# Batch 5's strided output goes through DRAM with an earlier deadline, and the Exp parts beside MM2 groups are spread out again

## The chip, the cores and the metric

The kernel runs on one core of a Trainium2 chip. A core has a matrix engine (TensorE, written PE in the profile, with its weight loads as PEld), a vector engine (DVE), a scalar engine (ACT), a general engine (POOL), and a sync engine (SP) that issues most DMAs here. Each engine runs its own instructions in order; they wait for one another through semaphores. The metric is the device time of one execution in microseconds (us); lower is better. Verdicts come from several runs of both kernels on one chip.

## What is computed

An attention with 8 heads over 8 batches of 576 positions, followed by a two-layer network with a squared ReLU:

```
B, H, S, D = 8, 8, 576, 64          # inputs q, k, v, float32
mask_local   = (rel >= 0) & (rel < 32)                    # heads 0 to 3, rel = i - j
mask_strided = (rel >= 0) & (j % 32 == i % 32)            # heads 4 to 7
attn = softmax(where(mask, q @ k.T / 8, -1e9));  o = attn @ v
x   = o as [B*S = 4608, H*D = 512]
h   = x @ w_in                      # w_in  512 x 2048
out = (max(h, 0) ** 2) @ w_out      # w_out 2048 x 512
```

The kernel leaves out all score blocks that a mask makes empty: a local row sees its own block of 96 and the 32 keys before it; a strided row sees only the 18 keys of its class modulo 32, so 4 classes make a block of 72.

## The kernel before

**Units.** A unit `u` is one batch and one pair of heads; batch b has units 4b to 4b+3. The first two are local, the last two strided. The output of a pair fills one of the four arrays `xt[0..3]` (128 rows of two heads, 4608 columns of positions), which is the transposed x that the network reads. `xt[2]` and `xt[3]` hold the strided pairs; batch b's columns are 576b to 576b+575.

**Steps of a unit.** `step_T` transposes q or k on PE (early batches only; later ones come transposed by DMA). `step_S` makes the scores: four banks of PSUM out of the five of pool `ps_t`, then four Exp parts on ACT (`expo(row, half)`) and two mask multiplications on DVE (`masks(row)`). `step_D` multiplies by v, in two or three parts, and scales by the row sums, giving `x_l` or `x_s` in SBUF, with positions on the partitions. Last, this x must be transposed into `xt`. There are three ways: `step_E` on PE with a copy by DVE or ACT (L449 to L460); for local pairs from batch 2 on a DMA transpose from SBUF (L444); and for strided pairs for which `by_dram` holds, `step_X`: SP writes `x_s` to a DRAM tile `x_d` (L471), and six groups later SP issues a DMA transpose from there to `xt` (L473).

**Groups.** The network is cut into nine chunks of 512 columns, and each chunk into 16 pieces of MM1 (`mm1`: four matmuls, one on each `xt[kk]` in turn, then ReLU on ACT and the square on DVE) and 16 of MM2 (`mm2`: four matmuls; every fourth one ends with a copy of y on ACT and a store on SP). These 288 pieces, of four matmuls each, are the groups; they are listed in a fixed order. Chunks 0, 1 and 2 have their 16 MM1 groups, and chunks 0 and 1 their 16 MM2 groups, in stretches of one kind; from chunk 3 on MM1 of one chunk alternates with MM2 of the chunk before. MM2 of chunks 0 and 1 are groups 16 to 31 and 48 to 63. MM1 of chunk c from 3 on starts at group 80 + 32(c-3); chunk 5 starts at group 144, chunk 6 at 176.

**The plan.** The attention steps are spread over the groups so that batch b's are done by a deadline. Batch b must be there when chunk b starts. The deadline is two groups before that, or 14 groups before for batches from XD on; this is read from the constant `XD` in two places:

```
    def by_dram(u):
        return not is_local(u) and units[u][0] >= XD
...
        g_end, s_end = ready.get(b, starts[b] - (14 if b >= XD else 2)), ends[4 * b + 3]
...
        if b + 2 < B:
            plan(b + 2, g_end + 2, g_prev, g_end)
```

So the deadlines are groups 110, 142, 162 and 194 for batches 4, 5, 6 and 7. The last line hangs the loads of batch b+2 on the same stretch: `loads_qk` at 45% of it (loads of local q and k by SP, casts of strided q and k to DRAM by POOL's DMAs, casts by POOL), `transpose_str` (SP's two DMA transposes of strided q and k, which wait for those casts) at 80% of it or 8 groups after the first, `transpose_local` (two DMA transposes for each local pair) 14 and 18 groups after the first, and `loads_v` two groups after the deadline (four DMAs for local v, two for strided v, and POOL's casts).

**The parts of a score step.** `later(n, ...)` puts work n groups off. Normally the four Exp parts and the masks of a pair are spread over four groups, so that ACT can serve the ReLUs between them. In the kernel before, `free_act` is set in MM2 groups of chunks 0 and 1, where there are no ReLUs; a score step there issues its four Exp parts at once, and its masks one and two groups later.

Of the kernel before, what the change touches and what calls it, by code (L numbers as in the profile page):

```python
# [14 lines left out]
def kernel(  # L15
# [79 lines left out]
    def is_local(u):  # L95
        return units[u][1] < H // 4
# [140 lines left out]
        nc.gpsimd.dma_start(out=w_out_b[:, c, :], in_=w_out_v[:, c, :])  # L237

    clock = [0]
    free_act = [False]  # L240
    pending = []

    def later(n, fn, key=None):
        pending.append((clock[0] + n, key, fn))
# [8 lines left out]
    def tick():  # L253
        clock[0] += 1
        run_due(lambda x: x[0] <= clock[0])
# [36 lines left out]
    def step_S(u):  # L292
        s = st[u]
        qT, kT = s["qT"], s["kT"]
        local = is_local(u)
        w, n = (QL, NL) if local else (SP_, NJ)
        kn = 128 if local else SP_
        hn = n // 2
        e = es[u % 4]
        s["e"] = e  # L300
        banks = [[None, None], [None, None]]
        for half in range(2):
            for row in range(2):
                banks[row][half] = ps_t.tile([128, 512], FP32, name="pt")
            for i in range(hn):
                t = half * hn + i
                klo = w * t
                for row in range(2):
                    rows = slice(64 * row, 64 * row + 64)
                    if not local and units[u][0] >= XB:  # L310
                        c0 = w * (t // 4)
                        lhsT, rhs = (a[rows, t % 4, c0:c0 + w] for a in (kT, qT))
                    else:
                        lhsT, rhs = kT[rows, klo:klo + kn], qT[rows, w * t:w * (t + 1)]
                    nc.tensor.matmul(banks[row][half][0:kn, w * i:w * (i + 1)], lhsT, rhs,  # L315
                                     start=True, stop=True)

        def expo(row, half):
            lo = S * row + S // 2 * half
            nc.scalar.activation(e[0:kn, lo:lo + S // 2], banks[row][half][0:kn, 0:S // 2],  # L320
                                 AF.Exp, scale=scale)

        def masks(row):
            x = e[0:kn, S * row:S * (row + 1)].rearrange("p (t c) -> p t c", c=w)
            m = mask_loc if local else mask_str
            nc.vector.tensor_tensor(x, x, m.to_broadcast([kn, n, w]), op=ALU.mult)  # L326
            if u < 2:
                nc.vector.memset(x[0:32, 0], 0.0)

        s["masks"] = masks  # L330
        if units[u][0] == 0:
            for row, half in ((0, 0), (0, 1), (1, 0), (1, 1)):
                expo(row, half)
            return
        if free_act[0]:
            for row, half in ((0, 0), (0, 1), (1, 0), (1, 1)):
                expo(row, half)
            later(1, lambda: masks(0), u)
            later(2, lambda: masks(1), u)
            return  # L340
        expo(0, 0)
        later(1, lambda: expo(0, 1), u)
        later(2, lambda: (masks(0), expo(1, 0)), u)
        later(3, lambda: expo(1, 1), u)
        later(4, lambda: masks(1), u)
# [114 lines left out]
                                  px.rearrange("c (j p) -> c p j", j=NJ))  # L460
        st.pop(u)

    XD = 6

    def by_dram(u):
        return not is_local(u) and units[u][0] >= XD

# [11 lines left out]
    def mm1(c, ff, kks=range(4), order=range(4), pool=None):  # L479
        if ff == 0 and c not in gs:  # L480
            gs[c] = g_pool.tile([128, 16, 512], BF16, name="g_sb")
        g = gs[c]
        if kks[0] == order[0]:
            phs[ff] = ph_tile() if pool is None else pool.tile([128, 512], FP32, name="py")
        ph = phs[ff]
        for kk in kks:
            nc.tensor.matmul(ph, w_in_b[:, kk, 128 * ff:128 * (ff + 1)],  # L487
                             xt[kk][:, 512 * c:512 * (c + 1)],
                             start=(kk == order[0]), stop=(kk == order[-1]))
        if kks[-1] != order[-1]:  # L490
            return
        r = r_pool.tile([128, 512], BF16, name="r")
        nc.scalar.activation(r, ph, AF.Relu)  # L493
        later(1, lambda: nc.vector.tensor_tensor(g[:, ff, :], r, r, op=ALU.mult))  # L494
# [3 lines left out]
    def mm2(c, i, pool=None):  # L498
        j, part = divmod(i, 4)
        g = gs[c]  # L500
        if part == 0:
            ys[c, j] = ps_y.tile([128, 512], FP32, name="py") if pool is None else ph_tile()
        py = ys[c, j]
        for ff in range(4 * part, 4 * part + 4):
            nc.tensor.matmul(py, g[:, ff, 128 * j:128 * (j + 1)], w_out_b[:, ff, :],  # L505
                             start=(ff == 0), stop=(ff == 15))
        if part == 3:
            y = y_pool.tile([128, 512], FP32, name="y")
            r0 = 512 * c + 128 * j
            if r0 + 128 == T:  # L510
                nc.vector.tensor_copy(y[:, 0:256], py[:, 0:256])
                nc.scalar.copy(y[:, 256:512], py[:, 256:512])
                nc.sync.dma_start(out=out[r0:r0 + 128, 0:256], in_=y[:, 0:256])
                nc.scalar.dma_start(out=out[r0:r0 + 128, 256:512], in_=y[:, 256:512])
                return
            nc.scalar.copy(y, py)  # L516
            nc.sync.dma_start(out=out[r0:r0 + 128, :], in_=y)

    T_ = lambda u, nm: (lambda: step_T(u, nm))
    S_ = lambda u: (lambda: step_S(u))  # L520
    D_ = lambda u, part: (lambda: step_D(u, part))
    E_ = lambda u: (lambda: step_E(u))
# [12 lines left out]
    def first_steps():  # L535
# [14 lines left out]
        for item in (("T", a, "q"), 2, ("T", a, "k"), 2, ("T", b, "q"), ("S", a), 1, ("T", b, "k"), 2, ("S", b),  # L550
                     ("M", a), 1, ("T", c, "q"), ("T", c, "k"), 1, ("N", a), ("S", c), 1, ("M", b), ("N", b), 1,
                     ("T", d, "q"), ("T", d, "k"), 2, ("S", d), 1, ("M", c), ("N", c), ("O", b), 1, ("X", b),
                     ("O", a), 1, ("M", d), ("X", a), ("N", d), ("O", c), ("X", c), ("P", (b, a), (0,)), ("O", d),
                     ("P", (b, a), (1, 2)), ("X", d), ("P", (c,)), ("P", (d,))):
            if isinstance(item, int):
                warm(item)
                continue
            op, u = item[0:2]
            if op == "T":
                step_T(u, item[2])  # L560
            elif op == "S":
                step_S(u)
            elif op == "M":
                masks(u)
            elif op == "N":
                step_N(u)
            elif op == "O":
                outs(u)
            elif op == "X":
                scaled[u]()  # L570
            else:
                part(*item[1:])
# [128 lines left out]
    groups = []  # L701
    starts = {}
    weights = []
    only_mm2 = []

    def add(c, kind, i, pool=None):
        only_mm2.append(kind == 2 and c < 2)
        if kind == 0:
            groups.append(lambda: None)
            weights.append(3)  # L710
        elif kind == 1:
            if i == 0:
                starts[c] = len(groups)
            groups.append(lambda: mm1(c, i))
            weights.append(3 if c < 3 else 5)
        else:
            groups.append(lambda: mm2(c, i, pool))
            weights.append(7 if c < 2 else 5)

    def mm1_alone(c):  # L720
        for i in range(16):
            add(c, 1, i)

    for ff in range(16):
        add(0, 1, ff) if ff >= NP else add(0, 0, ff)
    for part in range(4):
        for j, pool in ((0, ps_h), (1, ps_h), (2, None)):
            add(0, 2, 4 * j + part, pool)
# [35 lines left out]
    for b in range(1, B):  # L764
        g_end, s_end = ready.get(b, starts[b] - (14 if b >= XD else 2)), ends[4 * b + 3]
        if b == 1:
# [6 lines left out]
        done_prev, g_prev = s_end, g_end  # L773
    done = 0
    for n, g in enumerate(groups):
        free_act[0] = only_mm2[n]
        while done < due[n]:
            steps[done]()
            done += 1
        for fn in hooks.get(n, ()):  # L780
            fn()
        g()
        tick()
# [32 lines left out]
```

## Time and profile before

| what | value |
|---|---|
| median of 3 runs | 314.05 us (313.89 to 314.37) |
| the profiled execution, its own time | 314.05 us |
| its span, from first to last instruction | 312.3 us |
| granted TensorE clock, mean | 1.000 |
| matmuls of MM1 (L487) and MM2 (L505) | 576 + 576, 379 ns each as recorded, overlapping |
| Exp parts (L320) | 128, 407 ns each |
| PE transposes of x (L451) | 80 of strided x, 12 of local x |
| copies of strided xt by DVE (L459) | 6, 750 ns each |
| writes of x_d (L471), issue on SP | 4, 309 to 334 ns |
| transposes from x_d (L473), issue on SP | 4, 1175 to 1187 ns |

A recorded matmul of 379 ns overlaps its neighbours: four of them, one group, follow each other in 0.86 us on the chain. The chain of waits is the way to read this kernel: for each stretch it tells what the next instruction waited for. SP's own timeline tells when each DMA was issued; its "us" are the issue alone, not the transfer.

### The profile page before, as it was taken

The page shows a single profiled execution, that of the slowest core. Times are in us where ns is not written, and L with a number is a line of the kernel's source. Part 1 is how long each engine was busy: PE and PEld are TensorE (multiplying, and loading weights), DVE is VectorE, ACT ScalarE, POOL GpSimd, SP SyncE. Part 2 cuts the span into 40 slices and gives each one's busy share as a digit, 9 for nine tenths or more (in the row PEclk, how much of TensorE's full clock was granted, in tenths as well). Part 3 has the DMA queues.
Part 4 walks back from the last instruction along what each step waited for, and adds up shares of the span by engine and source line. Part 5 has one row for each costly group of instructions (what it writes and reads, how often), then busy time and mean ns, then how long its engine had stood idle before and what let it go on. Part 6 is the DMA issues. An engine that isn't in the chain of part 4 may idle for free.

```text
span 312.3 us, 6165 instructions
## 1 busy us (share of the span) xinstructions
PE 299.5 (96%) x2352; PEld 146.8 (47%) x2352; DVE 165.9 (53%) x411; ACT 162.3 (52%) x337; POOL 90.6 (29%) x117
## 2 busy tenths in 40 slices
PE   8889899999999999999999999999999999999994
PEld 3544455545554544444444454444444444444441
DVE  7676656578766866577466657654432222222200
ACT  3966554577555765555555555555444444444311
POOL 8518852727730633291057025000000000000000
PEclk9999999999999999999999999999999999999999
DMA  7999999999999999999899885224132000000111
GB/s 142 157 206 221 206 191 246 190 283 232 182 179 206 199 222 171 185 239 234 165 208 214 168 186 112 73 71 55 52 93 66 34 37 34 34 34 36 67 67 67
DMA packets 92172, 44.99 MB, mean 144 GB/s; under 512 B 76592, under 2 KB 85456, under 8 KB 91952
## 3 DMA queue, kind: packets, MB, share of 16 engines
q1 hardware_dynamic: 77120, 34.09, 51.2%
q0 software_dynamic: 14880, 10.39, 22.7%
q8 instruction: 18, 0.29, 0.4%
q10 hardware_dynamic: 144, 0.13, 0.1%
q14 instruction: 10, 0.08, 0.1%
HBM read 36.70 MB, written 13.57 MB: 161 GB/s over the span
## 4 chain that ended last, share of the span: by engine, by line
PE 76%; DMA 9%; DVE 6%; POOL 5%; issue 1%; ACT 1%; DVEq 0%; POOLq 0%; ACTq 0%
PE ph L487 32%; PE py L505 27%; PE ph L505 9%; DMA w_in_b<-in_moe_w_in_dram 4%; PE pt L419 3%; DMA qT_s<-in_q_dram 3%; PE pt L315 3%; DVE x_s L434 2%; DMA kTl<-k_l 1%; DVE g_sb L494 1%; PE pt L451 1%; POOL vs L227 1%; DVE e L326 1%; DVE kTl L286 1%; ACT r L493 1%
## 5 line engine op out<-in xcount | busy, mean ns | idle before, releaser
L487 PE MATMUL ph<-xt,w_in_b 128*128 128x512 bf16 x572 | 143.7, 379 | 0.3 <-ACT r L493 0.3
L493 ACT ACTIVATE r<-ph 128x512 bf16<-128x512 f32 x143 | 85.3, 597 | 94.6 <-PE ph L487 93.7
L494 DVE TENSOR_TENSOR g_sb<-r 128x512 bf16<-128x512 bf16 x144 | 69.9, 488 | 106.0 <-ACT r L493 105.1
L505 PE MATMUL py<-w_out_b,g_sb 128*128 128x512 bf16 x400 | 102.7, 379 | 0.0
L487 PEld LDWEIGHTS <-w_in_b 128*128 128x128 bf16 x576 | 52.3, 98 | 56.4 <-issue 0.5
L505 PEld LDWEIGHTS <-g_sb 128*128 128x128 bf16 x576 | 52.4, 98 | 55.2
L320 ACT ACTIVATE e<-pt 128x288 bf16<-128x288 f32 (+1 forms) x128 | 46.4, 407 | 14.8 <-PE pt L315 14.7
L505 PE MATMUL ph<-w_out_b,g_sb 128*128 128x512 bf16 x176 | 42.8, 379 | 0.0
L419 PEld LDWEIGHTS <-e 128*128 128x128 bf16 (+1 forms) x392 | 20.8, 97 | 15.9 <-issue 0.6
L192 POOL CAST vl<-vl_st 128x768 bf16<-128x768 f32 x12 | 10.6, 880 | 50.5 <-DMA vl_st<-in_v_dram 42.4
L434 DVE TENSOR_TENSOR x_s<-pt,rinv 72x384 bf16<-72x384 f32 (+1 forms) x42 | 21.4, 509 | 1.4
L326 DVE TENSOR_TENSOR e<-e,mask_str 72x576 bf16<-72x576 bf16 x32 | 17.1, 539 | 6.0 <-ACT e L320 5.9
L123 POOL CAST q_l<-q_st 96x768 bf16<-96x768 f32 x14 | 12.3, 877 | 24.8 <-DMA q_st<-in_q_dram 14.8
L326 DVE TENSOR_TENSOR e<-e,mask_loc 128x576 bf16<-128x576 bf16 x32 | 16.8, 525 | 3.5 <-ACT e L320 3.3
L516 ACT COPY y<-py 128x512 f32<-128x512 f32 x25 | 14.7, 587 | 5.5 <-PE py L505 5.5
L123 POOL CAST k_l<-k_st 96x768 bf16<-96x768 f32 x14 | 13.6, 974 | 11.6 <-DMA k_st<-in_k_dram 9.7
L434 DVE TENSOR_TENSOR x_l<-pt,rinv 96x384 bf16<-96x384 f32 x28 | 15.5, 553 | 1.0
L433 DVE RECIPROCAL rinv<-pt 96x6 f32<-96x6 f32 (+2 forms) x70 | 12.8, 183 | 5.1 <-PE pt L419 4.8
L516 ACT COPY y<-ph 128x512 f32<-128x512 f32 x10 | 5.9, 590 | 17.0 <-PE ph L505 17.0
L208 POOL CAST vs<-v_st 72x1024 bf16<-72x1024 f32 x12 | 14.0, 1197 | 0.4
L419 PE MATMUL pt<-vs,e 72*128 72x65 bf16 x224 | 13.1, 193 | 0.0
L530 PE MATMUL py<-y 128*128 128x512 bf16 x24 | 9.5, 485 | 1.3 <-DVE y L659 1.3
(87 smaller groups left out, 157.7 us busy)
## 6 DMA issues: line engine op xcount, KB each, us to landing
out_dram<-y SPq DMA_DIRECT2D x35, 256.0 KB, 3.4
vl_st<-in_v_dram SPq DMA_DIRECT2D x24, 144.0 KB, 3.9
v_st<-in_v_dram SPq DMA_DIRECT2D x12, 288.0 KB
q_st<-in_q_dram SPq DMA_DIRECT2D x16, 144.0 KB, 4.3
k_st<-in_k_dram SPq DMA_DIRECT2D x16, 144.0 KB, 6.8
w_in_b<-in_moe_w_in_dram POOLq DMA_DIRECT2D x4, 512.0 KB, 12.5
w_out_b<-in_moe_w_out_dram POOLq DMA_DIRECT2D x4, 512.0 KB, 10.8
q_st<-in_q_dram SPq DMA_DIRECT2D x7, 288.0 KB, 8.5
```

Source lines behind the costliest of these rows:

```text
L123: copy(t.rearrange("p j h d -> p h j d"), s[name + "f"].rearrange("p h (j d) -> p h j d", j=6))
L208: (copy or nc.gpsimd.tensor_copy)(t[:, :, 0:D], s["vf"].rearrange("p h (j d) -> p (h j) d", d=D))
L320: nc.scalar.activation(e[0:kn, lo:lo + S // 2], banks[row][half][0:kn, 0:S // 2], AF.Exp, scale=scale)
L326: nc.vector.tensor_tensor(x, x, m.to_broadcast([kn, n, w]), op=ALU.mult)
L419: nc.tensor.matmul(po[:, n - n0, :], e[0:kn, pos(n):pos(n) + 128], rhs[0:kn, src(n), 0:D + 1], start=True, stop=True)
L433: nc.vector.reciprocal(rinv[0:w, 0:m], po[0:w, 0:m, D:D + 1])
L434: nc.vector.tensor_tensor(x, po[0:w, 0:m, 0:D], rinv[0:w, 0:m].to_broadcast([w, m, D]), op=ALU.mult)
L487: nc.tensor.matmul(ph, w_in_b[:, kk, 128 * ff:128 * (ff + 1)], xt[kk][:, 512 * c:512 * (c + 1)], start=(kk == order[0]), stop=(kk == order ...
L493: nc.scalar.activation(r, ph, AF.Relu)
L494: later(1, lambda: nc.vector.tensor_tensor(g[:, ff, :], r, r, op=ALU.mult))
L505: nc.tensor.matmul(py, g[:, ff, 128 * j:128 * (j + 1)], w_out_b[:, ff, :], start=(ff == 0), stop=(ff == 15))
L516: nc.scalar.copy(y, py)
```

## The change

```
@@ the spreading of Exp parts and masks
-    free_act = [False]
...
-        if free_act[0]:
-            for row, half in ((0, 0), (0, 1), (1, 0), (1, 1)):
-                expo(row, half)
-            later(1, lambda: masks(0), u)
-            later(2, lambda: masks(1), u)
-            return
         expo(0, 0)
         later(1, lambda: expo(0, 1), u)
         later(2, lambda: (masks(0), expo(1, 0)), u)
         later(3, lambda: expo(1, 1), u)
         later(4, lambda: masks(1), u)
@@ the way of strided x
-    XD = 6
+    XD = 5
@@ the list of groups, and the loop over them
-    only_mm2 = []
...
-        only_mm2.append(kind == 2 and c < 2)
...
-        free_act[0] = only_mm2[n]
```

The first part is undone everywhere: score steps beside MM2 groups of chunks 0 and 1 (seven of them, of batches 1 and 3) spread their parts like all others. The second part moves units 22 and 23 (batch 5, strided) from `step_E` to `step_X`, and batch 5's deadline from group 142 to 130. With it the steps of batch 5 lie in groups 110 to 130 and those of batch 6 in 130 to 162 (before 110 to 142 and 142 to 162). The loads of batch 7, which hang on batch 5's stretch, move too: `loads_qk` from group 124 to 119, `transpose_str` from 135 to 127, the two `transpose_local` from 138 and 142 to 133 and 137, `loads_v` from 144 to 132. Nothing changes in what is computed. POOL's instructions keep their order.

## The prediction

> **What bounds the kernel now.** I read first the shares and slices of the page:
>
> ```profile
> PE 299.5 (96%) x2352; PEld 146.8 (47%) x2352; DVE 165.9 (53%) x411; ACT 162.3 (52%) x337; POOL 90.6 (29%) x117
> PE   8889899999999999999999999999999999999994
> DMA  7999999999999999999899885224132000000111
> ```
>
> PE has no free slice from 120 us to its end at 308 us, so there a step on PE costs its length and a wait of PE is lost for good. The DMA engines are full until about 170 us. Next the chain of waits, in the stretch where batch 5 ends:
>
> ```profile
> 167.49 0.26 PE pt L451 x8
> 175.63 0.26 PE pt L451 x8
> 177.62 0.18 PE pt L419 x6
> 177.80 0.86 PE ph L487 x4
> 179.71 0.40 PE pt L315 x16
> ```
>
> All pieces are PE's. The two L451 rows are step E of units 22 and 23. Counting four matmuls to a group, the L487 at 177.80 is group 144, the first MM1 of chunk 5, which reads batch 5's xt. Then SP's timeline, since the new DMAs go through SP in order:
>
> ```profile
> 155.97 1.21 SPq L444 DMA_TRANSPOSE xt<-x_l  x1
> 157.28 0.53 SPq L517 DMA_DIRECT2D out_dram<-y  x1
> 157.86 1.40 SPq L107 DMA_DIRECT2D q_st<-in_q_dram  x2
> 163.10 1.38 SPq L107 DMA_DIRECT2D k_st<-in_k_dram  x2
> 164.57 1.26 SPq L444 DMA_TRANSPOSE xt<-x_l  x1
> 165.94 0.54 SPq L517 DMA_DIRECT2D out_dram<-y  x1
> 170.78 1.61 SPq L161 DMA_TRANSPOSE qT_s<-q_d  x1
> 172.60 1.28 SPq L161 DMA_TRANSPOSE kT_s<-k_d  x1
> 173.97 0.53 SPq L517 DMA_DIRECT2D out_dram<-y  x1
> 174.60 1.24 SPq L173 DMA_TRANSPOSE qT<-q_l  x1
> 180.46 3.22 SPq L185 DMA_DIRECT2D vl_st<-in_v_dram  x4
> 183.73 1.16 SPq L201 DMA_DIRECT2D v_st<-in_v_dram  x2
> ```
>
> Between 152.78 and 185 SP has one gap of over 0.3 us: from 166.5 to 170.78 it stands before batch 7's transpose of strided q. SP's list of waits says why, and the list of tile x_d gives the landing of the new kind of transfer:
>
> ```profile
> SPq L161 <- DMA q_d<-in_q_dram: 4.3, 1, 4.3
> DMA to landing us min/median/max: 2.6/2.6/2.6
> ```
>
> **The change, part by part.** *PE work removed.* Two E steps of 8 transposes at 0.26 (chain): -0.5 us, all on the bound. Their two DVE copies (0.75 each) lie beside PE work and are worth nothing.
>
> *Work moved on PE.* Batch 5's steps in 20 groups instead of 32, batch 6's in 32 instead of 20: the same work. Before, batch 6 had the tight 20, from group 142 at 175.9 to 196, and PE was busy 18.00 of 18.00 us from 178 to 196 in the windows. I take 0. The inputs of the advanced steps are there: group 134, where unit 24 now needs v, falls at about 168, and POOL cast that v at 156.7 to 158.4. If one came late by under the stall found below, that would hide it.
>
> *Exp spread out in MM2 groups.* In the timeline of batch 1 (36 to 42 us) the second pair's scores stand at 39.25, its Exps take 1.32 and unit 4's product with v ends at 41.73, after a wait of 0.48 for POOL's v. Spread, the next q transpose takes the bank of the second pair's first Exp and waits 0.4 for it; the first pair's last Exp stands behind that q's copy on ACT (0.67), then come Exp 0.33 and mask 0.46. So that product ends at about 42.1 to 42.2: +0.4 to +0.5. Later in the stretch a mask moves behind the x_s that the PE transpose waits for (at 53.3 and 53.8), about -0.2. Batch 3's score steps lie further from their users; I find no new wait of PE there. This small delay has a cover:
>
> ```profile
> 110.58 0.43 PE L315 MATMUL pt<-kT,kTl 64*128 64x96 bf16 x12 [0.62 <-DMA kTl<-k_l]
> ```
>
> There PE waits 0.62 for a transpose that SP issued at 106.21, in a row that SP works off without a gap since 87.21; a PE that is up to 0.6 late waits less. I take 0, with bounds of -0.2 and +0.5 if the cover is gone (the row of SP would then have been waiting for PE).
>
> *DMAs on SP.* Added: two x_d writes (0.32 to issue) and two transposes from x_d (1.18). Advanced: all loads of batch 7. What counts is what stands before them. By the groups of the code SP's new order is: xt of unit 20, eight loads of q and k, a store, xt of unit 21, write of x_d 22, the two strided q/k transposes of batch 7, a store, write 23, transpose 22, six loads of v, two local transposes, a store, transpose 23. The strided pair still can't go before 170.78: it waits for POOL's cast to DRAM, issued at 165.51 behind POOL's casts of batch 6's v, which wait for loads that SP issues at 152.78, ahead of every moved entry. So the hold of 4.3 us stays, and behind it now stands the transpose that chunk 5 needs. From 170.78, with the durations above: pair to 173.9, store to 174.5, write 23 to 174.9, transpose 22 to 176.2 (landing 2.6 later, at 177.6 or more), four v loads 2.1 to 3.2 (rows at 152.78 and 180.46), two more 0.9 to 1.2, two local transposes 2.6, store 0.6. Transpose 23 is issued at 182.4 to 183.8. Landing: 2.6 in x_d's quiet rows near 200 us, 4.4 as the median of xt<-x_l on the page, under load. So it lands at 185.0 to 188.2; I take 186.7.
>
> *When PE wants it.* Group 144 was at 177.80. Done before it in addition: the scores of unit 26 (0.40) and three parts of products (0.18 each), less 0.52: 178.2. MM1's fourth matmul, on xt[3], comes 0.65 later: 178.9. So a new wait of 186.7 - 178.9 = 7.8 us, between 6.1 and 9.3. PE runs in order, so everything behind waits too; ACT and DVE run dry; no slack follows, for PE is full to the end.
>
> *The matmul rate after the wait.* No row has PE idle so long in mid-kernel (longest 1.3). At the start, the first eight 512-column matmuls, from 1.26 us, take 3.60 us (0.43 apart), against 0.22 within a group later; two more at 5.40 still take 0.99, two at 6.48 only 0.60. So a fresh start costs up to half of about 4.9 us, 2.4; the other bound is 0. An 8 us wait is nearest to the start, so I take 2.4. [...]
>
> Sum: -0.5 + 0 + 0 + 7.8 + 2.4 = +9.7. The profiled execution took 314.05 with a span of 312.3 (1.75 around it) and equals the median; the forecast is 314.05 + 9.7 = 323.8 us.
>
> **Rivals.** (1) *In time, so faster.* If SP reached transpose 23 by 176, it would land under the first matmuls of chunk 5 and only the 0.5 is left: 313.5 us. For it: x_d's transposes of batch 6 were issued at 197.44 and 203.30, well before chunk 6 at 210, with the same 14 groups. Against it: after 196 SP has gaps of several us and no loads left; at 170 it has 12 us of issue between the hold and transpose 23. It decides from 7.8 us earlier on.
>
> (2) *A half wait.* If advanced loads shift POOL's cast or its landing 4 us forward, SP's whole row moves with it: a wait of 7.8 - 4 = 3.8, too short, I suppose, to lose the rate: 314.05 - 0.5 + 3.8 = 317.4. For it: the hold is a DMA's landing (5.3 us from 165.51), which varies with load. Against it: POOL's order and the loads it waits for are unchanged up to there.
>
> (3) *No wait and no cover.* Transposes in time, but the spread Exps cost their 0.5 in full: 314.05 - 0.5 + 0.5 = 314.05, no change.
>
> **How the numbers follow.** The forecast 0.90; rival 1 0.04; rival 2 0.04; rival 3 0.02. About 0.2% is what a measurement here tells from no change. Only rival 1 is faster by more, only rival 3 within: 0.04, 0.02, and 0.94 slower. The forecast's own bounds: 6.1 - 0.5 - 0.2 + 0 = +5.4 and 9.3 - 0.5 + 0.5 + 2.4 = +11.7, so 319.4 to 325.8. The launch rate may need longer than at the start, since it depends on when PE resumes; I add 1.2 above: 327.0. So the range is 319.4 to 327.0; it leaves out the rivals, 0.1, and a little of my own case.
>
> **What would show it.** Right: PE's list of waits gets one row of 6 to 9 us, L487 waiting for the transpose from x_d, near 179; matmuls right after it are 0.43 apart for some us; SP issues the second transpose of x_d past 182 and strided q again at about 170.8; the kTl wait at 110.6 shrinks. Wrong: no such row (rival 1), strided q issued before 168 (rival 2), or PE waits in groups 110 to 144 that push its arrival instead (the end would hardly move, the names would). My prediction falls altogether if SP can pass the hold.

## The result, and the profile after

The changed kernel is slower: a median of 326.14 us (324.43 to 328.15, 6 runs) against 313.97 us (313.12 to 314.37, 6 runs) of the kernel before on the same chip. The ratio is 1.0397, with a 95% interval of 1.0349 to 1.0444. Ratios here are of mean times, without executions in a slower state of the chip, and so need not be those of the medians. The forecast was 323.8 us, the range 319.4 to 327.0. The profiled execution took 326.61 us with a span of 324.9, which is 12.6 more than the execution profiled before.

The shares and slices of the page, of the changed kernel:

```profile
PE 301.7 (93%) x2336; PEld 147.1 (45%) x2336; DVE 165.3 (51%) x409; ACT 163.0 (50%) x337; POOL 91.4 (28%) x117
PE   8889898999899999999999169999999999999994
PEclk9999999999999999999999859999999999999999
DMA  7999999999999988999999971431124010000121
```

PE's count is 16 lower (the two E steps of 8). A slice is 8.1 us. PE has a hole in the 23rd and 24th slice, from 179 to 195 us, and there the granted clock is down too. The DMA engines are full until well into the hole, and after it they are not. PE's list of waits (total, times, longest) names the hole, and answers for the small wait that was to give cover:

```profile
PE ph L480 <- DMA xt<-x_d: 9.6, 2, 8.1
PE pt L314 <- DMA kTl<-k_l: 0.3, 1, 0.3
```

L480 is MM1, L487 of the listing before. SP's timeline (start, duration of the issue) shows how the transposes from x_d, L466, came to be late:

```profile
168.19 0.52 SPq L464 DMA_DIRECT2D x_d<-x_s  x1
171.38 2.73 SPq L161 DMA_TRANSPOSE qT_s<-q_d  x1
174.65 1.28 SPq L161 DMA_TRANSPOSE kT_s<-k_d  x1
...
177.09 1.20 SPq L466 DMA_TRANSPOSE xt<-x_d  x1
178.38 2.29 SPq L185 DMA_DIRECT2D vl_st<-in_v_dram  x4
...
185.11 1.21 SPq L466 DMA_TRANSPOSE xt<-x_d  x1
```

The order is the one that the prediction reads from the code. SP stands from 168.71 to 171.38 for the casts of strided q and k to DRAM by POOL's DMAs, loses some more at the second of the pair, and then works without a gap of over half a us until transpose 23 goes out at 185.11. What PE did meanwhile, from its timeline (the bracket is idle time before the row, and what ended it):

```profile
181.21 0.38 PE L480 MATMUL ph<-xt,w_in_b 128*128 128x512 bf16 x1 [1.53 <-DMA xt<-x_d]
189.67 0.58 PE L480 MATMUL ph<-xt,w_in_b 128*128 128x512 bf16 x1 [8.09 <-DMA xt<-x_d]
...
190.82 1.89 PE L498 MATMUL py<-w_out_b,g_sb 128*128 128x512 bf16 x4
...
194.05 1.03 PE L498 MATMUL py<-w_out_b,g_sb 128*128 128x512 bf16 x4
```

These are the third and the fourth matmul of the first MM1 of chunk 5, whose first two, on the local pairs, began at 179.08. The third waits for transpose 22 and the fourth for transpose 23. The two groups from 190.82 to 194.05 then take 1.68 and 1.55 us, where 0.86 is a group at full rate. The windows show the clock (after the stretch and its length: busy PE, PEld, DVE, ACT and POOL with their instructions, then the granted clock, DMA share and GB/s):

```profile
182.00:184.00 2.00, 0.00 (x0) 0.00 (x0) 0.00 (x0) 0.00 (x0) 1.09 (x2) 0.91 1.80 219
...
192.00:194.00 2.00, 2.00 (x6) 0.76 (x5) 0.00 (x0) 0.00 (x0) 0.00 (x0) 0.53 0.39 92
```

In the windows left out, from 184 to 192, the clock is 0.50, and after 194 it is 1.00. By the two shown it fell at about 183.6, so when PE starts again at 189.67 it goes on at half rate until about 193.9. From the resuming matmul to the start of the group at 194.05 it takes 4.38 us for one matmul (0.22), the scores (0.40) and two groups (0.86 each), 2.34 at full rate: 2.0 us are lost on top of the wait. The chain of waits ties it together (pieces of it in order of time):

```profile
167.19 7.45 DMA k_d<-in_k_dram
...
185.11 4.52 DMA xt<-x_d
```

The cast of strided k to DRAM lands 7.45 us after its start and lets SP go on at 174.65; transpose 23 takes 4.52 us from issue to landing, and PE resumes at 189.67. Between the two the chain runs along SP's row, for a part of it by way of a load of v and POOL's cast of that.

### The profile page after: what moved, and what is told of

It reads as the page before. It is cut to its first block, busy times and chain, and to the rows that moved or that the text cites. A ratio compares the mean times of both kernels' runs of the same rounds, so it can differ in the third digit from the quotient of the medians.

```text
span 324.9 us, 6145 instructions
## 1 busy us (share of the span) xinstructions
PE 301.7 (93%) x2336; PEld 147.1 (45%) x2336; DVE 165.3 (51%) x409; ACT 163.0 (50%) x337; POOL 91.4 (28%) x117
## 4 chain that ended last, share of the span: by engine, by line
PE 62%; DMA 20%; POOL 5%; DVE 5%; SPq 3%; issue 2%; ACT 1%; POOLq 0%; DVEq 0%; ACTq 0%
PE ph L480 27%; PE py L498 23%; PE ph L498 8%; DMA vs<-in_v_dram 4%; DMA w_in_b<-in_moe_w_in_dram 4%; DMA qT_s<-in_q_dram 3%; PE pt L314 2%; PE pt L412 2%; DMA k_d<-in_k_dram 2%; DMA vl_st<-in_v_dram 2%; DVE x_s L427 2%; DMA k_st<-in_k_dram 2%; SPq L173 1%; DMA xt<-x_d 1%; DMA kTl<-k_l 1%
## 5 line engine op out<-in xcount | busy, mean ns | idle before, releaser
L480 PE MATMUL ph<-xt,w_in_b 128*128 128x512 bf16 x572 | 144.9, 381 | 9.9 <-DMA xt<-x_d 9.6
L487 DVE TENSOR_TENSOR g_sb<-r 128x512 bf16<-128x512 bf16 x144 | 68.7, 479 | 117.9 <-ACT r L486 117.2
L480 PEld LDWEIGHTS <-w_in_b 128*128 128x128 bf16 x576 | 52.7, 98 | 59.2 <-issue 3.4
L319 ACT ACTIVATE e<-pt 128x288 bf16<-128x288 f32 (+1 forms) x128 | 47.4, 407 | 13.7 <-PE pt L314 13.6
L192 POOL CAST vl<-vl_st 128x768 bf16<-128x768 f32 x12 | 11.5, 956 | 53.8 <-DMA vl_st<-in_v_dram 40.1
L325 DVE TENSOR_TENSOR e<-e,mask_loc 128x576 bf16<-128x576 bf16 x32 | 19.6, 613 | 2.4 <-ACT e L319 2.4
L123 POOL CAST q_l<-q_st 96x768 bf16<-96x768 f32 x14 | 13.2, 944 | 23.5 <-DMA q_st<-in_q_dram 14.6
L314 PEld LDWEIGHTS <-kT_s 64*72 64x72 bf16 x192 | 4.6, 118 | 13.7 <-issue 13.1
```

The costliest lines, as they stand in the source:

```text
L123: copy(t.rearrange("p j h d -> p h j d"), s[name + "f"].rearrange("p h (j d) -> p h j d", j=6))
```

## Experiments: which part of the change costs it

**The first part alone.** The Exp parts spread out, batch 5 as before.

```
 (changed kernel)
-    XD = 5
+    XD = 6
```

> Only the first part of the change: Exp parts and masks spread everywhere, batch 5 as before. Theory (queue): the part is worth nothing or little, 0 with bounds of -0.2 and +0.5 us against the kernel before, since PE's wait of 0.6 near 110 us covers it. Rival (spread costs): the changed kernel's PE reached group 78 about 1.0 us later than before (113.0 against 112.0), and nothing gives it back, so +1.0 us. If it is slower by several us, the new wait isn't the main cost.

Measured: 314.15 us (313.58 to 317.87) against 315.05, a ratio of 1.0002 (0.995 to 1.0054). The span of its profile was 311.9, 0.4 below that of before. PE's kTl wait near 110 was 0.90 there, 0.62 before and 0.3 in the changed kernel; it moves both ways between executions (1.39 in a second profile of the changed kernel, below). The spreading costs nothing that can be seen; the interval still allows some 1.5 us either way, so its bounds of -0.2 to +0.5 are not told apart.

**The second part alone.** The Exp parts at once, as before; strided x of batch 5 by DRAM.

```
 (kernel before)
-    XD = 6
+    XD = 5
```

> Only the second part: batch 5 by DRAM with the earlier deadline, Exp parts at once as before. Theory: the whole loss but at most 1 us of it is here, +10 to +12 us against the kernel before, with one wait of MM1 for the second transpose from x_d of 6 to 10 us. Rival: the two parts only hurt together, then this stays within 2 us of before.

Measured: 327.67 us (325.71 to 329.18), a ratio of 1.0401 (1.0343 to 1.0458), the same as the whole change. PE's waits for the transposes from x_d were 2.75 and 8.52 us, and SP issued transpose 23 at 187.17. The whole loss lies in the second part.

**The deadline alone.** Batch 5 is 14 groups earlier, its strided x still transposed by PE.

```
 (kernel before)
-... ready.get(b, starts[b] - (14 if b >= XD else 2)), ...
+... ready.get(b, starts[b] - (14 if b >= 5 else 2)), ...
```

> The kernel before with batch 5's deadline 14 groups early and nothing else: its strided x still goes by PE. Theory: the same PE work in another order, no wait of PE, 0 within 0.4 us of the kernel before. Rival (the packed stretch of 20 groups beside full DMA engines makes PE wait): over 1 us slower.

Measured: 314.95 us (312.78 to 315.7, 12 runs) against 314.79, a ratio of 0.9989 (0.9965 to 1.0013). Packing batch 5's steps and advancing batch 7's loads cost nothing while no MM1 depends on what SP issues behind them.

## Experiments: what holds transpose 23

**The loads of v out of the way.** Batch 7's six loads of v go eight groups later, so that transpose 23 is issued ahead of them; the hold stays.

```
 (changed kernel)
-        at(n0, lambda: loads_v(b))
+        at(n0 + (8 if b == 7 else 0), lambda: loads_v(b))
```

> The changed kernel with only batch 7's six loads of v put off from group 132 to 140, behind the second transpose from x_d; the hold stays in front. Theory: SP issues that transpose 3 to 3.5 us earlier, near 181.7, the wait is 5 to 7 us in place of 9.6 and the rate may still fall: 3 to 5 us faster than the changed kernel, 321 to 323. Rival (the hold alone counts): no gain; rival (the loads alone count): 8 us or more.

Measured: 322.37 us (321.22 to 324.44), a ratio of 1.0239 (1.0195 to 1.0283), some 4 us better than the changed kernel. Transpose 23 went out at 182.30, 2.8 earlier, though the strided pair began 1.9 later (173.28): counted from there it took 9.0 in place of 13.7. It also landed sooner: PE went on at 184.89, 2.6 after the issue, where the changed kernel had 4.5. PE's timeline of this run:

```profile
181.59 0.38 PE L480 MATMUL ph<-xt,w_in_b 128*128 128x512 bf16 x1 [1.76 <-DMA xt<-x_d]
184.89 0.58 PE L480 MATMUL ph<-xt,w_in_b 128*128 128x512 bf16 x1 [2.92 <-DMA xt<-x_d]
...
186.03 1.89 PE L498 MATMUL py<-w_out_b,g_sb 128*128 128x512 bf16 x4
...
190.49 0.35 PE L412 MATMUL pt<-vs,e 72*128 72x65 bf16 x6
```

The waits are 4.7 in all, and still the three groups from 186.03 to 190.49 take 4.46 us in place of 2.58: even this much shorter wait loses the rate. From 184.89 to 190.49 it is 5.60 for one matmul, the scores and three groups, 3.20 at full rate: 2.4 us lost.

**The hold out of the way.** Batch 7's transposes of strided q and k go nine groups later, behind transpose 23; the loads of v stay ahead of it.

```
 (changed kernel)
-        at(max(g + 8, ...), lambda: transpose_str(b))
+        at(max(g + 8, ...) + (9 if b == 7 else 0), lambda: transpose_str(b))
```

> The changed kernel with batch 7's two transposes of strided q and k issued from group 136 in place of 127, after the second transpose from x_d; the six loads of v stay ahead of it. Theory (the hold for POOL's cast stands in front): SP goes on at 168.7, the second transpose is issued near 177 and lands near 181, the wait shrinks to 1 to 3 us and the matmul rate stays, so about 8 us faster than the changed kernel, 316 to 318. Rival (the transfers themselves are late, or SP has too many entries whatever their order): less than 3 us faster.

Measured: 328.45 us (327.06 to 328.91), a ratio of 1.0421 (1.037 to 1.0473). That is a miss: no gain at all. SP's list of waits says what took the place of the hold, and its timeline when:

```profile
SPq L466 <- DMA x_d<-x_s: 6.5, 1, 6.5
```

```profile
170.75 0.51 SPq L464 DMA_DIRECT2D x_d<-x_s  x1
172.18 0.44 SPq L464 DMA_DIRECT2D x_d<-x_s  x1
179.17 1.18 SPq L466 DMA_TRANSPOSE xt<-x_d  x1
...
186.87 1.98 SPq L466 DMA_TRANSPOSE xt<-x_d  x1
```

The first transpose from x_d is now free of the casts, but must wait until its own write of x_d has landed, which it does only at about 179.1: 8.4 us after that write, the first of the two, was issued. (It isn't the second that it waits for: in the changed kernel transpose 22 follows write 23 by 0.44 without a wait.) So the hold for POOL's cast had hidden a second wait in the same place, about as long. All that followed it in the changed kernel, the loads of v and the two local transposes, still follows, and transpose 23 goes out at 186.87, 16.1 us after the write of unit 22, where the changed kernel had 16.9. This row was also late from its start: that write went out at 170.75, and at 168.19 in the changed kernel.

**Both out of the way.** Batch 7's loads and local transposes go back to the groups that they had before (`loads_v` at 144, `loads_qk` at 124), and the strided pair to 136, so that both transposes from x_d go ahead of them.

```
 (changed kernel)
+        if b == 7:
+            n0, g1 = n0 + 12, g1 + 12
...
-        at(max(g + 8, ...), lambda: transpose_str(b))
+        at(max(g + 8, ...) + (b == 7), lambda: transpose_str(b))
```

> The changed kernel with batch 7's loads hung where they were before (groups 124, 138, 142 and 144) and its strided transposes at 136, so that both transposes from x_d of batch 5 are issued ahead of the hold. Theory (queue order is all of it): no wait of MM1 for x_d, clock 1.00, -0.5 for the two PE transposes and up to +1 for the spread Exps: 313.5 to 315. Rival (going by DRAM is itself slow or loads the DMA engines): still over 317.

Measured: 315.26 us (314.07 to 317.21, 12 runs) against 314.79, a ratio of 1.0015 (0.9991 to 1.0039). The loss of 12 us is gone, with the deadline, the way by DRAM and the spread Exps all kept. SP's waits and timeline, then PE's list:

```profile
SPq L466 <- DMA x_d<-x_s: 7.4, 2, 5.3
```

```profile
169.51 0.68 SPq L464 DMA_DIRECT2D x_d<-x_s  x1
175.57 1.17 SPq L466 DMA_TRANSPOSE xt<-x_d  x1
...
177.47 1.31 SPq L466 DMA_TRANSPOSE xt<-x_d  x1
```

```profile
PE ph L480 <- DMA xt<-x_d: 1.8, 1, 1.8
```

The write of unit 22 holds SP here too, for 5.3 us, as the chain of waits has it:

```profile
168.41 7.10 DMA x_d<-x_s
```

But only a store stands between the two transposes. Transpose 23 goes out at 177.47, 7.6 earlier than in the changed kernel, and PE waits 1.8. After it the scores take 0.40 and the next group 0.87: the rate is kept, and the granted clock over the span is 0.999. What the two E steps save, 0.5, is less than the 1.8, so nothing is won.

**The same mend with the Exp parts at once.**

```
 (the mended kernel above)
+        if free_act[0]:
+            for row, half in ((0, 0), (0, 1), (1, 0), (1, 1)):
+                expo(row, half)
...
```

> As the one before, but with the Exp parts at once beside MM2 groups, as in the kernel before: batch 5 by DRAM, queue mended. Theory: 0.5 us faster than the kernel before (two times eight PE transposes gone, no wait), 313.5. Rival: the packed stretch of batch 5 costs what the transposes save, no change or slower.

Measured: 315.05 us (313.88 to 318.46, 12 runs), a ratio of 1.0033 (0.9994 to 1.0072), with 2.0 us of PE's waits for x_d. It can't be told from the kernel before, nor from the run above.

## Experiments: the rate after the wait

**Keeping PE busy, first try.** 40 matmuls that nobody needs stand between MM1's second and third matmul at the start of chunk 5.

```
 (changed kernel, in mm1)
+            if c == 5 and ff == 0 and kk == 2:
+                pw = ps_y.tile([128, 512], FP32, name="py")
+                for _ in range(40):
+                    nc.tensor.matmul(pw, w_in_b[:, 0, 0:128], w_in_b[:, 0, 0:512], start=True, stop=True)
```

> The changed kernel with 40 idle matmuls of 512 columns (results unused) on PE ahead of the third matmul of chunk 5, where PE would stand still. Theory (the matmul rate falls in the wait): at 0.216 each they fill 8.6 of the 9.6 us of waiting, the clock stays at 1.00, and the kernel is about 2 us faster than the changed one, near 324. Rival (the wait alone costs, the rate afterwards is nothing of its own): no change from the changed kernel, 326, or some tenths more.

Measured: 326.45 us (324.39 to 329.63), a ratio of 1.0344 (1.0274 to 1.0413). In the execution profiled, the longest of the four, transpose 23 was issued only at 188.38; the unneeded matmuls ended at 190.6, PE then waited another 2.13, and the two groups behind that were at half rate again. It didn't do what it was made for, and says nothing on the cost of the rate.

**Second try, with the changed kernel beside it.** First the changed kernel again:

> The changed kernel again, as the measure for the two runs beside it. Both theories: 1.035 to 1.045 of the kernel before, a longest wait of PE for the transpose from x_d of 7 to 10 us near 180, the clock granted 0.97 to 0.985 over the span, because the matmuls that follow the wait run at half rate for some 4 us.

Measured: 325.61 us (323.51 to 328.62) against 314.38, a ratio of 1.0348 (1.0302 to 1.0394). In its profile (span 322.2, an execution of 323.92, so below the median) transpose 23 was issued at 183.25 and PE waited once, for 7.7:

```profile
187.50 0.58 PE L480 MATMUL ph<-xt,w_in_b 128*128 128x512 bf16 x1 [7.72 <-DMA xt<-x_d]
...
191.38 1.03 PE L498 MATMUL py<-w_out_b,g_sb 128*128 128x512 bf16 x4
```

The same count as above gives 191.38 - 187.50 - 2.34 = 1.5 us lost to the rate. Then the same kernel with 42 unneeded matmuls, now between the third and the fourth:

```
 (changed kernel, in mm1)
+            if c == 5 and ff == 0 and kk == 3:
+                pw = ps_y.tile([128, 512], FP32, name="py")
+                for _ in range(42):
+                    nc.tensor.matmul(pw, w_in_b[:, 0, 0:128], w_in_b[:, 0, 0:512], start=True, stop=True)
```

> The changed kernel with 42 unneeded matmuls (w_in by itself, into a bank that nobody reads) between MM1's third and fourth matmul at the start of chunk 5, where the long wait lies: at 0.22 us each 9.2 us of PE work inside a wait of 8.1 us, so that PE is never idle for more than some tenths. Theory (the half rate after the wait costs 2.1 us beside the wait itself): granted clock 0.995 or more, matmuls after the wait 0.22 apart from the first on, and 2.1 less the overrun of some 1.0 gained, so 1 us under the changed kernel's median, up to 2 where the transpose lands later. Rival (PE's rate after the wait doesn't set the end, since other engines have to start again too): no gain, or 1 us worse through the overrun.

Measured: 326.51 us (324.46 to 328.72), a ratio of 1.039 (1.0351 to 1.0428): no gain. In its profile PE waited 2.34 for transpose 22, ahead of the unneeded matmuls, with no other wait near it, and the clock went to half: at 0.71 over 182 to 184, in the next window (columns as above):

```profile
184.00:186.00 2.00, 2.00 (x6) 0.75 (x5) 0.00 (x0) 0.00 (x0) 0.94 (x2) 0.50 1.47 214
```

By the next window, of 0.94, it came back at about 186.2. So the 42 took 10.6 us from their first start to the fourth matmul's instead of 9.2, and ran over the landing: PE's wait for it is gone, and how much was overrun can't be seen. An estimate: transpose 23 went out at 188.19, and with the 2.6 to 4.6 us until PE goes on in the other profiles it could have gone on at 190.8 to 192.8, 0.9 to 2.9 before 193.74. Matmuls behind them were at full rate (the next groups 0.87 apart), but what that wins, the overrun seems to take. The rival reads this result as well as the theory does.

**The shorter wait, kept busy.** The loads of v eight groups later, as above, and 16 unneeded matmuls in the same place.

```
 (the run with the loads of v later, in mm1)
+            if c == 5 and ff == 0 and kk == 3:
+                ...
+                for _ in range(16):
```

> The changed kernel with batch 7's loads of v eight groups later, as in the run on the loads of v, and 16 unneeded matmuls (3.5 us) between MM1's third and fourth matmul at the start of chunk 5, where that run had a wait of 2.9 us after one of 1.8. Theory (a wait of about 2 to 3 us is enough for half rate, which cost that run 2.3 us on its three groups after the wait: 1.89, 1.9 and 1.24 against 0.86 each): granted clock 0.995 or more, no half rate after 185, 1.0 to 2.3 us under 322.4 on the same footing, a ratio of about 1.017 to 1.021. Rival (the rate after so short a wait does not decide): 1.024 or more.

Measured: 321.11 us (319.11 to 323.41), a ratio of 1.0206 (1.0162 to 1.025), against 1.0239 (1.0195 to 1.0283) without them. The groups after the fourth matmul, which started at 186.28, follow each other in 0.87. The rate was lost in this profile too, after a wait of 2.81 for transpose 22 (the clock is 0.65 over 180 to 182 and 0.50 over 182 to 184), but ahead of the unneeded matmuls, which paid for it: up to the fourth matmul they took 4.6 us in place of 3.5. The median lies within what the theory expected and under the rival's 1.024, but the two intervals overlap. What the rate costs is therefore read from the rows of the traces (2.0, 1.5, and 2.4 in the run on the loads of v); no run has shown it by the median alone.

## Why the prediction held, and where its sizes were off

The mechanism was right: a new wait of PE, at the place named (in the first profile in two pieces, since transpose 22 came late too), because transpose 23 stood behind the strided pair, six loads and two local transposes on SP. The size was 12.6 us in the profiled execution, where 9.7 were forecast. That the range held owes something to luck: the bounds of the forecast's own terms end at 325.8, and the median of 326.14 lies inside only by the 1.2 added for a slower rate. The rate didn't need it, with 2.0 and 1.5 lost in place of 2.4; SP's row and the landing did. No run shows that 1.2, nor that the rate depends on when PE resumes, which was a supposition: no loss read from a trace here is above 2.4. Term by term, with the second profile of the same kernel beside it:

| step of the prediction | forecast | first profile | second profile |
|---|---|---|---|
| strided pair issued on SP by | 173.9 | 175.9 | 173.9 |
| transpose 23 issued | 182.4 to 183.8 | 185.11 | 183.25 |
| from there until PE resumes | 2.6 to 4.4 | 4.6 | 4.3 |
| PE could have begun the fourth matmul | 178.9 | 179.7 | 179.6 |
| waits for x_d, in all | 7.8 | 9.6 | 7.7 |
| loss of rate after it | 2.4 | 2.0 | 1.5 |
| span, more than before | 9.7 | 12.6 | 9.9 |

*SP's row.* The step "the hold stays", with the row of 170.78 taken over, was the term mis-sized. The q cast let SP go on 0.6 later than before (171.38), and the k cast came late as well: the first of the pair took 2.73 us and the second could start only at 174.65, 2.05 past the 172.60 of before. From there on every duration used was within some tenths, so transpose 23 came 1.3 past the upper end. More than half of the 2.05 was there ahead of the hold. The prediction took SP's loads of batch 6's v, behind which POOL's casts stand, from the row of before, at 152.78. SP issued them here at 154.34, and POOL its casts of q and k 1.2 later than before (165.51 and 165.99 there), as the timelines of SP and POOL show:

```profile
154.34 2.15 SPq L185 DMA_DIRECT2D vl_st<-in_v_dram  x4
```

```profile
166.71 0.49 POOL L153 DMA_DIRECT2D q_d<-in_q_dram  x1
167.19 0.49 POOL L153 DMA_DIRECT2D k_d<-in_k_dram  x1
```

The rest is the landing of the k cast. In the second profile the loads of v stand at 152.78 again, the pair was through at 173.85, and transpose 23 went out inside the range. In the other profiles of runs that keep the pair in front, the loads of v went out at 153.8 to 156.5, the q cast at 166.5 to 169.5, and the pair began 5.2 to 6.8 after that (at 174.50 in the run of the second part, 175.44 in that of the 42 matmuls). So the whole row moves by some us between executions, more by what lies ahead of it on SP than by the landing of the casts, and the forecast took it from one execution, with the loads of v as early as in any. Why they come later in others I leave open.

*Landing.* The prediction took an arrival 2.9 to 4.3 after the issue. The traces give 4.5 in the first profile and 4.2 in the second, so the upper bound, the loaded xt<-x_l, was the better row.

*When PE wants it.* 0.8 and 0.7 later than forecast. PE was already late by 0.9 and 0.4 at group 78 (113.0 and 112.5 us, where 112.1 was before), long ahead of any part of batch 5. The spread Exps alone don't make it: in that run group 78 began at 111.6. It differs between executions, and I leave its cause open.

*PE work removed, and the packed stretch.* The first, -0.5, is too small to be seen by itself; the second, 0, is shown by the deadline alone (0.9989, 0.9965 to 1.0013). *The spread Exps* at 0 fit their run, which can't tell 0 from the bounds. The sign that the kTl wait near 110 would shrink didn't hold: 0.25 in the first profile, but 1.39 in the second, where 0.62 was before.

*The sum.* First profile: 0.9 late at group 144 beyond the forecast, 9.6 of waits, 2.0 of rate, less 0.5: 12.0 of the 12.6. Second: 0.8 + 7.7 + 1.5 - 0.5 = 9.5 of 9.9. The rest of about half a us I didn't trace. The 0.2% that the prediction would tell from no change was too fine: the intervals here are 0.24 to 0.69% either way.

*The rivals.* Rival 1 (in time) said it would decide from 7.8 us earlier on. The mended kernel puts transpose 23 7.6 earlier, and the loss is gone, which shows that what stood ahead of it on SP made the 12 us. (1.1 of them are a sooner landing, 3.5 after the issue in place of 4.6, now that the loads come later too.) It isn't faster, though: 1.8 of wait were left against 0.5 saved. Rival 2 (a half wait) supposed that 3.8 us would be too short to lose the rate. That is wrong: 4.7 in two pieces lost 2.4, and a single wait of 2.34 was followed by a clock of 0.50. By its terms with the rate, 314.05 - 0.5 + 3.8 + 2.4 = 319.8. *The sentence that I would take back* is that the prediction falls if SP can pass the hold: SP passed it in the run made for that, and the next wait, for x_d's own write, stood in the same place. The prediction had priced this write at its issue, 0.32, and not at its landing, 7 to 8 us there.

The loss of 2.0, 1.5 and 2.4 us in three profiles lies at or below the 2.4 that the prediction took from the start of the kernel, an estimate: half of the 4.9 us from the first 512-column matmul, at 1.26, to about 6.2, in its rows of PE. The half rate lasted 4.2, 3.2 and 5.0 us after PE's start in the three profiles, worked out from the windows' clock. The length of a wait alone did not decide whether the rate fell. Single waits of 2.13, 2.34 and 2.81 (in the runs with 40, 42 and 16 unneeded matmuls) were each followed by a clock of 0.50 in a window of 2 us. The 1.82 of the mended kernel was not, and neither was an earlier wait of the run with 40, after which the clock is 1.00 up to 44:

```profile
38.03 0.43 PE L270 MATMUL pt<-ident,q_l 96*128 96x96 bf16 x6 [2.63 <-POOL q_l L123]
```

And in the run on the deadline alone the clock was down at 20 us, though PE had no wait of over 0.8 us in the 6 us before:

```profile
20.00:22.00 2.00, 2.00 (x16) 0.94 (x15) 1.07 (x3) 0.14 (x1) 0.00 (x0) 0.50 1.24 206
```

## What to carry to other kernels

In the profiles here nothing on SP went ahead of an entry that waited (2.7 us for the q cast in the changed kernel, 6.5 for the write of x_d in the run without the hold): before a needed transfer is moved on to such a queue, list what stands ahead of it there, and take each wait at its worst landing under load, since one that is removed may only uncover the next. A row taken from one execution can stand some us later in the next. When loads hang on a deadline that is moved, they move in front of other work too; here a later place for them and for the transposes of strided q and k was worth 11 us and cost nothing. And a wait of PE can cost more than its length: here three of 2.1 to 2.8 us were followed by half rate, and one of 2.6 was not. So a small saving on PE is no fair price for a transfer that arrives near its deadline.

## What was not expected of the hardware

A write of x_d, 0.5 us to issue, landed 7.1 us after its issue in the mended kernel and 8.4 in the run without the hold. The share of the DMA engines in the windows of 2 us from the issue on was 1.55 falling to 0.61, and 1.79 falling to 0.53. What made it land so late no run here shows.

Transposes from x_d landed 2.6 us after issue near 200 us in the kernel before, and between 175 and 193 PE went on 2.6 to 4.9 after their issue. Where the clock fell to half at a wait for x_d, it did so between 1.0 and 4.1 us after PE's last matmul before the wait (183.0 after 181.97 in the run on the loads of v, where a wait of 1.76 lay just before, and 183.9 after 179.78 in the second profile of the changed kernel). The granted clock doesn't show the slow start of the kernel: it is 1.00 in all windows from 0 to 10 us of the kernel before, though the first eight matmuls took 3.60 us.
